# Idle identity products on TensorE in the planned waits at the start of an attention-and-two-layers kernel

## The chip, the cores and the metric

The kernel runs on one core of a Trainium2 chip. The metric is the device time of one execution in microseconds (us). Three runs of the kernel before took 609.23, 608.94 and 610.55 us, a median of 609.23. One further execution was recorded by the hardware profiler; it took 610.69 us, of which 608.5 lie between its first and its last instruction (the span). All rows below come from that one.

Names of engines: PE is TensorE (PEld its weight loads), DVE is VectorE, ACT is ScalarE, POOL is GpSimd, SP is SyncE, which here only issues DMAs.

## The reference

Attention over 2 batches of 8 heads, 768 positions of 64 numbers each: every query sees the keys nearer than 16 positions and, beside them, 24 summaries of blocks of 32 (the maximum of the keys, the mean of the values). Its output, 1536 rows of 512, goes through two dense layers of 2048 hidden units, one after the other.

```python
k_sum = k.reshape(B, H, nb, block, D).max(axis=3)
v_sum = v.reshape(B, H, nb, block, D).mean(axis=3)
scores_l = scale * np.matmul(q, k.transpose(0, 1, 3, 2))      # kept where |i - j| < 16
scores_s = scale * np.einsum('bhsd,bhnd->bhsn', q, k_sum) + np.log(block)
a = softmax(concatenate([scores_l, scores_s]))                 # in short
out = np.matmul(a, np.concatenate([v, v_sum], axis=2))
...
h = x @ w_in;  g = h * np.clip(h + 3.0, 0.0, 6.0) / 6.0;  x = g @ w_out
h = x @ w_in2; g = h * np.cos(h);                         x = g @ w_out2
```

## The kernel before

Two heads make a pair; attention works on a third of the positions (256) of one pair or, later, of two pairs at a time. One such unit is: a load of q (`z`), 16 or 32 small score products (line 538, tile `s`), mask and exponent on VectorE and ScalarE (lines 551 and 559, tile `e`), a normalising product (line 579), four transposes (line 589, tile `t`) and 16 or 32 products with v (line 600, tile `o`), whose result is split into a high and a low part, `xh` and `xl`. Before a pair's first unit its k and v are loaded, block maxima of k are taken, and block means of v are summed on PE (lines 492 and 500, tiles `h` and `y`) and copied into the tile `vw` (line 418 and 416). A float32 product is two records on PE in the trace.

The dense layers take 512 tokens by four groups of hidden units; each product with a weight is three passes (lines 702 to 704 for the first product, line 778 for the second). The weights are loaded raw, split into high and low parts on ScalarE, VectorE and GpSimd (lines 653, 657, 662, then 418 and 423, tiles `cf` and `w`), and the first of this work stands between the attention units.

Every piece of work is an operation with a priority and a cost per engine (`Plan.op`). `Plan.order` (line 252) plays the schedule through by these costs and fixes on which engine and at which planned time each operation starts; `Plan.run` (line 350) then writes the instructions in that order. On the chip each engine works through its own list in order and waits on semaphores, whatever the planned times were. In the planner's clock a product takes double its cost before 5 us (`T["cold"]`). Nine products of zeros (line 429, `warm=9`) stand ahead of everything on PE.

`Plan.run` can put idle products into the planned waits of PE: where the next operation of PE is planned to start later than the last one ends, it calls `self.idle()` (line 447), a product of the 128x128 identity with its own first 64 columns into a bank of `acc` that nothing reads before it is first used. It does so for waits that begin before `T["busy"]`, and no more once that bank is in use. `busy` is 0 before the change, so none is written.

Of the kernel before, what the change touches and what calls it, by code (L numbers as in the profile page):

```python
# [62 lines left out]
def consts():  # L63
# [13 lines left out]
T = dict(  # L77
    A0=5.118, AS=1.568, mask=-8.22, kp=-14.19, qp=-15.92, lk=-15.36, lq=-11.42, lv=-4.09, vs=37.77, vss=27.87,
    vsp=-18.03, wl=-15.78, wc=-15.19, g0=20.42, gi=5.51, pp=17.22, fill=-28.29, DVE=1.348, POOL=0.572, cold=5, d0=0.9,
    warm=9, tail=1, lagq=3, nraw=3, ncf=2, n=5, w2=2, n2=3, g2=3, nz=2, nr=1, busy=0, slack=0.2, vpe=-45.26,  # L80
    avg=-8.5,
)

# [38 lines left out]
class Plan:  # L122
# [227 lines left out]
    def run(self):  # L350
        self.refine()
        left, last, spare = self.first, T["cold"], True
        for o in self.order():
            if o.eng == "PE":
                if spare and last < T["busy"]:
                    for _ in range(int((o.start - last - T["slack"]) / (0.11 if last > T["cold"] else 0.22))):
                        self.idle()
                last = o.start + o.took
                spare = spare and not any(x.cls is self.spare and x.slot == 1 for x in o.uses)
            o.fn(o.eng)  # L360
            if o.seq < self.first:
                left -= 1
                if not left:
                    self.turn()
# [494 lines left out]
```

## Time and profile before

| | |
|---|---|
| median of three runs | 609.23 us (608.94 to 610.55) |
| profiled execution | 610.69 us |
| its span | 608.5 us |
| PE busy | 587.0 us, 96% of the span |
| VectorE, GpSimd, ScalarE busy | 386.0, 348.7, 268.1 us |
| mean granted clock of PE | 0.987 |

The granted clock is the share of 2.4 GHz that PE was given; 0.50 is its lower level, 1.2 GHz. A row of a timeline gives the start from the span's beginning, the length, engine, line, operation, what is written from what, and in brackets how long the engine was idle before it and what ended that. The records of products overlap: the distance between two starts is what one costs in a row of them.

### The profile page before, as it was taken

What the parts mean: (1) busy time and instruction counts of PE and PEld (TensorE: products, weight loads), DVE (VectorE), ACT (ScalarE), POOL (GpSimd) and SP (SyncE); (2) the same over time, 40 slices, a digit from 0 to 9 for tenths busy, and PEclk for the clock granted to TensorE, in tenths of its full rate; (3) what the DMA queues carried; (4) which work ended last, traced back from release to release, by engine and by line L of the source; (5) the groups of instructions that cost most, each with busy time, mean ns of one, the idle gap of its engine ahead of it and who ended that gap; (6) DMA issues with size and microseconds to landing.
All of it is one profiled execution on the core that took longest, in us unless ns stands there. A gap on an engine that the chain in (4) does not pass through costs nothing.

```text
span 608.5 us, 9274 instructions
## 1 busy us (share of the span) xinstructions
PE 587.0 (96%) x3482; PEld 486.0 (80%) x3482; DVE 386.0 (63%) x713; ACT 268.1 (44%) x567; POOL 348.7 (57%) x365
## 2 busy tenths in 40 slices
PE   4789899999999999999999999999999999999997
PEld 3569778788888888888888888888888888888885
DVE  4589964563952258523983689856994797575462
ACT  2878786543421114201440546654662363343240
POOL 1668864475843437623688498656763577443350
PEclk9879999999999999999999999999999999999999
DMA  9979930032410004300430013302330020000112
GB/s 245 295 226 273 256 124 18 2 139 70 138 70 0 1 22 152 103 1 0 152 125 1 1 69 105 103 1 70 104 103 2 0 104 0 1 1 1 69 53 87
DMA packets 28157, 50.05 MB, mean 82 GB/s; under 512 B 14288, under 2 KB 17744, under 8 KB 28112
## 3 DMA queue, kind: packets, MB, share of 16 engines
q1 hardware_dynamic: 27968, 49.40, 25.9%
q8 instruction: 27, 0.44, 0.3%
q14 instruction: 18, 0.15, 0.1%
q10 hardware_dynamic: 144, 0.07, 0.1%
HBM read 46.31 MB, written 3.15 MB: 81 GB/s over the span
## 4 chain that ended last, share of the span: by engine, by line
PE 88%; DMA 3%; POOL 3%; DVE 2%; ACT 2%; issue 1%; SPq 1%; DVEq 0%; ACTq 0%
PE acc L778 24%; PE s L778 18%; PE h L702 8%; PE h L703 8%; PE h L704 8%; PE t L703 3%; PE o L703 3%; PE o L704 3%; PE t L704 3%; PE o L702 3%; PE t L702 3%; DMA vw<-in_v_dram 2%; PE o L600 1%; PE s L538 1%; PE t L589 1%; ACT e L559 1%
## 5 line engine op out<-in xcount | busy, mean ns | idle before, releaser
L418 POOL TENSOR_SCALAR g<-r 128x512 fp32r<-128x512 f32 (+1 forms) x81 | 61.8, 764 | 127.4 <-DVE r L738 35.3
L423 POOL TENSOR_TENSOR g<-r,g 128x512 fp32r<-128x512 f32 (+1 forms) x83 | 111.8, 1347 | 8.6 <-ACT g L416 3.1
L734 ACT ACTIVATE n<-h,bias 128x512 f32<-128x512 f32 (+1 forms) x60 | 39.4, 656 | 138.7 <-PE h L704 138.6
L778 PE MATMUL acc<-g,w 128*128 128x512 f32 (+1 forms) x432 | 96.1, 370 | 0.6 <-POOL g L423 0.6
L702 PE MATMUL h<-xh,w 128*128 128x512 f32 (+1 forms) x240 | 92.3, 384 | 2.0 <-ACT xh L416 2.0
L703 PE MATMUL h<-xl,w 128*128 128x512 f32 (+1 forms) x240 | 90.9, 379 | 0.1
L704 PE MATMUL h<-xh,w 128*128 128x512 f32 (+1 forms) x240 | 90.6, 377 | 0.0
L778 PEld LDWEIGHTS acc<-g,w 128*128 128x128 f32 x432 | 75.1, 188 | 14.2 <-POOL g L423 0.8
L738 DVE SCALAR_TENSOR_TENSOR r<-n,h 128x512 f32<-128x512 f32 (+1 forms) x60 | 38.7, 645 | 50.9 <-POOL n L746 26.2
L423 POOL TENSOR_TENSOR w<-cf,w 128x512 fp32r<-128x512 f32 x46 | 67.3, 1466 | 3.6 <-ACT w L416 1.6
L778 PE MATMUL s<-w,g 128*128 128x512 f32 x288 | 69.2, 389 | 0.0
L778 PE MATMUL acc<-w,g 128*128 128x512 f32 x288 | 69.2, 389 | 0.0
L778 PEld LDWEIGHTS s<-w,g 128*128 128x128 f32 x288 | 54.1, 188 | 11.2
L778 PEld LDWEIGHTS acc<-w,g 128*128 128x128 f32 x288 | 54.1, 188 | 11.2
L653 ACT ACTIVATE cu<-raw 128x512 f32<-128x512 f32 x64 | 42.8, 672 | 39.9 <-DVE cf L662 27.2
L662 DVE SCALAR_TENSOR_TENSOR cf<-cu,cf 128x512 uint32<-128x512 uint32 x64 | 59.4, 943 | 1.1 <-ACT cu L653 0.5
L702 PEld LDWEIGHTS h<-xh,w 128*128 128x128 f32 x240 | 45.6, 190 | 11.0 <-ACT xh L416 2.2
L418 POOL TENSOR_SCALAR w<-cf 128x512 fp32r<-128x512 f32 x44 | 33.9, 774 | 34.2 <-DVE cf L662 24.8
L657 DVE TENSOR_SCALAR cf<-raw 128x512 uint32<-128x512 uint32 x64 | 45.0, 716 | 12.4 <-POOL w L423 9.1
L703 PEld LDWEIGHTS h<-xl,w 128*128 128x128 f32 x240 | 45.7, 190 | 8.6 <-DVE xl L423 0.7
L704 PEld LDWEIGHTS h<-xh,w 128*128 128x128 f32 x240 | 45.7, 190 | 8.1
L746 POOL TENSOR_SCALAR n<-n 128x512 f32<-128x512 f32 x36 | 26.3, 730 | 38.7 <-ACT n L734 38.6
(91 smaller groups left out, 1011.5 us busy)
## 6 DMA issues: line engine op xcount, KB each, us to landing
raw<-in_w_in_dram SPq DMA_DIRECT2D x32, 512.0 KB, 4.3
raw<-in_w_out_dram SPq DMA_DIRECT2D x32, 512.0 KB, 3.5
kw<-in_k_dram SPq DMA_DIRECT2D x8, 576.0 KB, 6.1
vw<-in_v_dram SPq DMA_DIRECT2D x8, 576.0 KB, 8.4
z<-in_q_dram SPq DMA_DIRECT2D x11, 256.0 KB, 5.8
out_dram<-part SPq DMA_DIRECT2D x8, 256.0 KB, 2.0
out_dram<-kw SPq DMA_DIRECT2D x3, 256.0 KB, 2.0
z<-in_q_dram SPq DMA_DIRECT2D x2, 128.0 KB, 5.5
```

Source lines behind the costliest of these rows:

```text
L418: eng[e].tensor_scalar(out=out, in0=in_, scalar1=scale, scalar2=0.0, op0=ALU.mult, op1=ALU.add)
L423: eng[e].tensor_tensor(out=out, in0=in0, in1=in1.bitcast(F32), op=ALU.subtract)
L653: lambda e, raw=raw, u=u: nc.scalar.activation(out=u.t, in_=raw.t.bitcast(F32)[:, :, 1], func=ACTF.Prelu, scale=2.0 ** -112, alpha=2.0 ** 32),
L657: lambda e, raw=raw, f=f: eng[e].tensor_scalar(out=f.t.bitcast(U32), in0=raw.t[:, :, 0], scalar1=2.0 ** -29, scalar2=7.0, op0=ALU.mult, op ...
L662: lambda e, u=u, f=f: nc.vector.scalar_tensor_tensor(out=f.t.bitcast(U32), in0=u.t.bitcast(U32), scalar=3, in1=f.t.bitcast(U32), op0=ALU.l ...
L702: nc.tensor.matmul(out=o, lhsT=wh, rhs=hi, start=(kk == 0), stop=False)
L703: nc.tensor.matmul(out=o, lhsT=wh, rhs=lo, start=False, stop=False)
L704: nc.tensor.matmul(out=o, lhsT=wl, rhs=hi, start=False, stop=(kk == KT - 1))
L734: op({"ACT": t(fixed, 0.43)}, lambda e: nc.scalar.activation(out=out(), in_=in_(), func=func, **kw), pr, r=rd, w=wr, take=take)
L738: op({"DVE": t(0.09, 0.56)}, lambda e: nc.vector.scalar_tensor_tensor(out=out(), in0=a(), scalar=s, in1=b(), op0=o0, op1=o1), pr, r=rd, w= ...
L746: op({"POOL": t(0.16, 0.47), "DVE": t(0.07, 0.265)}, lambda e: eng[e].tensor_scalar(out=n(), in0=n(), scalar1=1.0, scalar2=-MAGIC, op0=ALU ...
L778: nc.tensor.matmul(out=o, lhsT=l, rhs=r, start=(c == 0 and z == 0), stop=(c == GS - 1 and z == 2))
```

## The change

Two numbers. `busy` becomes 40, so idle products are written into the waits that begin before 40 us of the planned clock, and their number in each wait is worked out with a length of 0.26 us (0.46 in the first wait) in place of 0.11 (0.22).

```diff
-    warm=9, tail=1, lagq=3, nraw=3, ncf=2, n=5, w2=2, n2=3, g2=3, nz=2, nr=1, busy=0, slack=0.2, vpe=-45.26,
+    warm=9, tail=1, lagq=3, nraw=3, ncf=2, n=5, w2=2, n2=3, g2=3, nz=2, nr=1, busy=40, slack=0.2, vpe=-45.26,
...
                 if spare and last < T["busy"]:
-                    for _ in range(int((o.start - last - T["slack"]) / (0.11 if last > T["cold"] else 0.22))):
+                    for _ in range(int((o.start - last - T["slack"]) / (0.26 if last > T["cold"] else 0.46))):
                         self.idle()
```

In the program this makes 42 idle products, in eight places on PE: 8 before the first score, 15 before the first transposes, 3 before the third score, 6 before the first v sums, 5 before the first products with v, 1 before the score behind the second v sums, 1 and 3 around the products with v after it. The lists of the other engines and of the DMA queue are in the same order as before.

On PE, between the first score (`s` from k and q) and the transposes of its exponents (`t` from `e`), a piece of the difference:

```order
 L538 MATMUL s_130<-kw_92,z_84 64x120
 L538 MATMUL s_131<-kw_92,z_84 64x120
+L447 MATMUL acc_125<-ident 128x64 x15
 L589 MATMUL t_128<-ident,e_98 120x128 x4
 L538 MATMUL s_130<-kw_93,z_85 64x120
```

Fifteen products now stand where PE had nothing between the last score product and the first transpose; each transpose comes behind them on PE.

On PE, at the third piece of the dense layer's work (`h` from `xh`, `xl` and the weights `w`), with the products with v (`o`) and four transposes between:

```order
 L703 MATMUL h_127<-xl_72,w_112 128x256
 L704 MATMUL h_127<-xh_69,w_112 128x256
+L447 MATMUL acc_125<-ident 128x64
 L600 MATMUL o_129<-pt_102,vw_88 64x64 x8
 L600 MATMUL o_129<-pt_103,vw_89 64x64 x8
 L589 MATMUL t_128<-ident,e_99 120x128 x4
+L447 MATMUL acc_125<-ident 128x64 x3
 L702 MATMUL h_126<-xh_69,w_111 128x256
 L703 MATMUL h_126<-xl_72,w_111 128x256
```

One idle product now stands ahead of the products with v, and three between the transposes and the next product with `xh`.

## Rows read from the trace of the kernel before

**Rows 1.** The page, part 1: busy time, share of the span, instructions.

```profile
PE 587.0 (96%) x3482; PEld 486.0 (80%) x3482; DVE 386.0 (63%) x713; ACT 268.1 (44%) x567; POOL 348.7 (57%) x365
```

**Rows 2.** Stretches: busy time per engine (instructions), granted clock, DMA share, GB/s.

```profile
0.00:19.80 19.80, 11.33 (x126) 9.43 (x130) 8.98 (x48) 6.68 (x27) 3.75 (x14) 1.00 1.02 251
19.80:26.60 6.80, 3.92 (x74) 2.53 (x66) 3.50 (x18) 6.45 (x20) 5.65 (x7) 1.00 1.04 285
26.60:33.50 6.90, 5.90 (x72) 4.49 (x73) 3.98 (x12) 4.61 (x17) 3.45 (x6) 0.51 0.99 332
33.50:40.30 6.80, 4.66 (x79) 3.51 (x79) 6.65 (x10) 4.69 (x9) 5.37 (x5) 1.00 0.51 159
40.30:47.10 6.80, 6.55 (x69) 5.73 (x71) 5.25 (x27) 5.85 (x21) 4.88 (x7) 0.50 0.78 241
47.10:80.00 32.90, 30.53 (x483) 27.04 (x479) 29.82 (x104) 27.96 (x97) 28.19 (x36) 1.00 0.94 269
80.00:608.50 528.50, 524.10 (x2594) 433.27 (x2594) 327.81 (x498) 211.89 (x382) 297.38 (x295) 1.00 0.16 55
```

The engines in these rows are PE, PEld, DVE, ACT and POOL, in this order.

**Rows 3.** Timeline of PE, 1 to 51 us.

```profile
1.06 4.21 PE L429 MATMUL h<-n 128*128 128x128 f32 x18 [1.06 <-DVE n L427]
8.34 1.08 PE L538 MATMUL s<-kw,z 64*64 64x120 f32 x16 [3.07 <-DMA z<-in_q_dram]
12.91 1.08 PE L589 MATMUL t<-ident,e 128*120 128x128 f32 x4 [3.50 <-issue]
...
20.20 0.65 PE L589 MATMUL t<-ident,e 128*120 128x128 f32 x4
...
22.24 1.05 PE L538 MATMUL s<-kw,z 64*64 64x120 f32 x32
25.04 0.69 PE L600 MATMUL o<-pt,vw 120*64 120x64 f32 x16 [1.74 <-POOL vw L418]
...
27.08 1.51 PE L492 MATMUL h<-vw,avg 96*32 96x128 f32 x24 [0.78 <-DMA vw<-in_v_dram]
29.11 1.51 PE L492 MATMUL h<-vw,avg 96*32 96x128 f32 x24 [0.52 <-DMA vw<-in_v_dram]
...
40.40 0.58 PE L702 MATMUL h<-xh,w 128*128 128x256 f32 x1 [1.99 <-ACT xh L416]
...
43.99 1.88 PE L538 MATMUL s<-kw,z 64*64 64x120 f32 x32
...
50.01 0.63 PE L589 MATMUL t<-ident,e 128*120 128x128 f32 x4
```

**Rows 4.** The chain of waits in order of time: start, us, what.

```profile
16.97 12.10 DMA vw<-in_v_dram
29.07 0.04 issue
29.11 1.51 PE h L492 x24
...
42.99 0.21 PE h L703
...
47.97 0.12 PE h L704
```

**Rows 5.** Timeline of VectorE, its two waits for PE.

```profile
31.72 0.42 DVE L420 CAST xh<-o 128x256 fp32r<-128x256 f32 x1 [0.81 <-PE o L600]
...
45.92 0.28 DVE L551 CUSTOM_DVE_ANT_0 e<-s,mask 128x120 f32<-128x120 f32 x1 [1.32 <-PE s L538]
```

**Rows 6.** Timeline of ScalarE, its wait for PE.

```profile
47.58 0.60 ACT L416 ACTIVATE xh<-o 128x512 fp32r<-128x512 f32 x1 [1.35 <-PE o L600]
```

**Rows 7.** Timeline of GpSimd, 44 to 49 us.

```profile
44.59 0.20 POOL L571 TENSOR_SCALAR sm<-sm 128x4 f32<-128x4 f32 x1
...
47.50 1.15 POOL L579 TENSOR_TENSOR e<-e,sm 128x480 f32<-128x480 f32 x1
```

**Rows 8.** The page, part 5: PE's weight loads of line 702.

```profile
L702 PEld LDWEIGHTS h<-xh,w 128*128 128x128 f32 x240 | 45.6, 190 | 11.0 <-ACT xh L416 2.2
```

## The prediction

> **What bounds the kernel now.** I read the page's engine lines first [rows 1]. TensorE (PE) is busy 96% of the span, and nothing else is near that. Then I split the span where the granted clock changes and where PE's waits end [rows 2]: from 80.0 us to the end PE is busy 524.10 of 528.50 us at the full clock. Whatever makes PE enter that long stretch earlier or later moves the end by as much, and the change only touches what lies before 40 us of the planner's clock.
>
> In the first 47 us I went through PE's timeline, row by row with the waits [rows 3]. Two things limit PE there. One is data: it waits 3.07 us for q, 3.50 before the first transposes, 1.74 for the filled v, 0.78 and 0.52 for two v loads and 1.99 for xh. The other is its clock. The granted clock reads 0.50 from 26.6 to 33.5 and again from 40.3 to 47.1 [rows 2], the lower level, 1.2 GHz. Before its first fall the column reads 1.00, but the durations contradict it: four transposes take 1.08 us at 12.91 and 0.65 at 20.20, and 16 score products take 1.08 at 8.34 where 32 take 1.05 at 22.24 [rows 3]. So PE starts at 1.2 GHz too, and reaches 2.4 at about 20 us. Both falls come after PE had waited: the first behind the 1.74 and just before the end of the 0.78, the second at the end of the 1.99 [rows 3].
>
> **The price of an idle product.** Nothing in the trace is a 128x128 by 128x64 product. The nearest row is the warm-up: 18 records (two to a product) of 128 columns in 4.21 us [rows 3], 0.468 us a product at the low level, half of it, 0.234, at the high one. With half the columns it costs between half of that and all of it. A load of 128 columns of weights takes 190 ns whatever follows [rows 8], near the 234 ns of a record, and the idle product loads the same 128 columns; so I take the upper ends, 0.468 and 0.234. (The code itself counts with 0.46 and 0.26.)
>
> **Part by part.** The added products are 8, 15, 3, 6, 5, 1, 1 and 3, 42 in all; every other instruction stands on its engine where it stood, and no DMA moves.
>
> *The 8 before the first score.* Warm-ups end at 1.06 + 4.21 = 5.27, q lets the score start at 8.34. At the low level 8 x 0.468 = 3.74, to 9.01: the score 0.67 late. If the clock rises half way, 4 x 0.468 + 4 x 0.234 = 2.81, to 8.08, in time. What waits for that score (VectorE, then ScalarE, then SyncE's next load of q) shifts with it.
>
> *The 15 before the first transposes.* The wait is 3.50. At the high level 15 x 0.234 = 3.51 just fills it; at the low one 15 x 0.468 = 7.02, and the transposes start at 5.27 + 3.74 + 1.07 + 7.02 = 17.1 instead of 12.91, 4.2 late. This is the one place where the change can do harm.
>
> *The 3, the 6 and the 5.* They stand between the second score and the first o products, 14 x 0.234 = 3.3 us, 6.6 at the low level. What they stand ahead of ends, as the next paragraph shows, in a wait for data. Between those first o products and the last of the v sums PE waits 0.78 + 0.52, and ahead of them 1.74 [rows 3]: 3.0 us of slack against 3.3, so nothing at the high level; at the low one they add to the third rival.
>
> *Why an early clock brings nothing by itself.* The DMA engines' share is 1.02, 1.04 and 0.99 in the three stretches up to 33.5 [rows 2]. In the chain of waits a v load issued at 16.97 is in flight for 12.10 us, and the v sums on PE start at 29.11, 0.04 after it lands [rows 4]. All that PE gains before 29 ends in that wait. So I put the early part at 0, from both sides: nothing gained, and a loss only if the delay is longer than the slack there (the rival below).
>
> *The first low stretch, 26.6 to 33.5.* If PE were at 2.4 GHz there, the v sums (1.51 from 29.11) would end 0.75 earlier and the o products behind them more; VectorE waited 0.81 for that o [rows 5], so 0.8 is all that can be got. But the order puts no idle product between the transposes behind the first o products and the v sums, nor between the two v loads: the plan has those waits too short, and 0.78 and 0.52 stay open, or grow. I take 0, with 0.8 as the bound.
>
> *The second low stretch, 40.3 to 47.1.* Three idle products go into the 1.99 us wait just before it: 0.7 us of work, 1.4 at most, in a wait that ends with ScalarE's xh: free. If they keep the clock up, PE does 40.4 to 47.5 faster: 9 products of 256 columns at 0.12 each instead of 0.21 [rows 4] (0.8), four transposes 0.65 instead of 1.08 (0.4), the score 1.05 instead of 1.88 (0.8): 2.0 by the end of the score. Two thirds can be used. VectorE waits 1.32 for that score [rows 5], ScalarE 1.35 for the o products behind it [rows 6]; GpSimd runs from 44.59 without a wait, and its product that ends at 48.65 feeds the transposes at 50.01 [rows 7, 3]. All three caps say 1.3. From there to 80 us the four engines are busy 85 to 93% [rows 2], PE most, so 1.3 is passed on. Bounds: 0 if the clock falls anyway, 1.3.
>
> *The two single products* (one before the score behind the second v sums, one before the o products that follow) cost 0.23 each, 0.5 in all. They fall between 33 and 38, where VectorE is busy 6.65 of 6.80 us [rows 2] and everything waits for it. Nothing, with 0.5 as the bound.
>
> **The sum.** 0 - 0 - 1.3, against the profiled execution's 610.69 (span 608.5 and 2.2 around it), is 609.4. The median of the three runs is 609.23, 1.46 below the profiled one, and the runs fall into 608.94, 609.23 and 610.55: the distance between them is about what the second low stretch is worth. If the median run had that stretch, it goes to 607.9; if it hadn't, it stays near 609.2. I take 608.8.
>
> A page says the same of the clock: the Trainium skill, "TensorE: Matmul & The Clock Gate", in Part 1, states that the moment at which the clock rises varies from run to run of the same kernel, since it isn't tied to the kernel's start. The three times are compatible with that, no row here shows the clock of more than one run. By that rule the gain of 1.3 is a gain in some runs alone, and half of it, some 608.6, would be the median's.
>
> **The rivals.**
> 1. *The clock does as before.* The idle products stream few columns for their time, the clock still falls at 27 and 40, and they only fill waits. For it: they fill 0.7 of 1.99. Then 609.2.
> 2. *The clock stays up throughout.* For it: with the five products 1.2 of the 1.74 wait is filled. Against: the unfilled waits for v. 0.8 + 1.3 = 2.1 off: 607.1 from the median, 608.6 from the profiled run.
> 3. *Slower: the idle products run at 1.2 GHz and hold up the first transposes.* The 15 decide. If the clock isn't up when they start, the transposes come 4.2 late, and ScalarE, busy 6.45 of 6.80 us behind them [rows 2], passes that on: the o products go from 25.04 to 29.2, the v sums start at 30.5 rather than 27.08, and end at 30.5 + 2 x 0.75 = 32.0 with the clock up by then or 30.5 + 2 x 1.51 = 33.5 without, where they ended at 30.62: 1.4 to 2.9 late. VectorE already waits for them, so the end moves too: 609.23 + 1.4 to 2.9 is 610.6 to 612.1, 611.4 in the middle. For it: even the warm-up, 4.21 us of dense work, didn't raise the clock for the score at 8.34, and an idle product is less dense than that. Against: now it would be at work without a break from 1.06 on, and all three rises in the trace (about 20, 33.5 and 47.1) came while PE was at unbroken work.
>
> **Chances.** Forecast (second low stretch gone, the first not) 0.42; rival 1 0.22; rival 2 0.13; rival 3 0.23. A measurement of this kernel can't tell less than about 0.3%, 1.83 us. Faster than 607.4 needs rival 2 from the median (0.08) or the forecast with a spare 0.5 (0.04): 0.12. Slower than 611.06 is the upper half of rival 3 (0.13) and a little for what I don't see (0.03): 0.16. The rest, 0.72, is no change. The range 607.2 to 611.5 leaves out the upper quarter of rival 3 and the best of rival 2; the forecast's own is 607.9 to 609.4.
>
> **What would show it.** Right: transposes before 13.2 us with idle products of about 0.23 to 0.26 ahead of them; the v sums still starting near 29.1; a granted clock of 1.00 through 40 to 47; VectorE's 1.32 and ScalarE's 1.35 waits gone; PE's long stretch from 80 unchanged in length. Wrong: idle products of 0.46 ahead of the transposes, which then start at 17; a v load that lands earlier than 29.07, since then the early clock would pay after all; or a clock that falls at 40 in spite of the three products.

## The result: 0.75% slower, and the profile after

The changed kernel takes 613.98 us (612.93 to 615.01, 4 runs) where the kernel before, beside it, takes 609.09: a ratio of 1.0075, with a 95% interval of 1.0051 to 1.0099. A second measurement, the last of the experiments, gave 1.0024 (0.9997 to 1.0051), so the size of the loss is less sure than this first one makes it look. Ratios and intervals here and below go over all the fast runs and can differ from the quotient of the two medians; one execution of the kernel before, 843.52 us in the last batch, is slow and left out. The forecast was no change at 608.8, with a range of 607.2 to 611.5. The third rival came in, and cost more than it was given. The profiled execution took 613.61 us, 2.92 more than the one of before; that one, 610.69, is slower than each of the four runs of the kernel before, so the medians lie further apart (4.89) than the two profiles.

The page's first part says that PE has more instructions, and no other engine has:

```profile
PE 599.0 (98%) x3566; PEld 498.2 (81%) x3566; DVE 386.8 (63%) x713; ACT 268.3 (44%) x567; POOL 349.5 (57%) x365
```

Against [rows 1] that is 84 records more, the 42 products, and 12.0 us more of PE's time; the span grew by 3.0. The stretches show where those 3.0 lie. I cut again where the granted clock changes; the columns are those of [rows 2].

```profile
4.90:8.35 3.45, 2.08 (x22) 1.97 (x25) 1.97 (x5) 0.00 (x0) 0.80 (x4) 1.00 1.18 290
8.35:28.80 20.45, 20.45 (x178) 17.28 (x182) 7.57 (x44) 8.53 (x37) 5.14 (x10) 0.50 0.96 249
28.80:45.90 17.10, 13.92 (x230) 11.40 (x223) 16.22 (x47) 14.26 (x36) 13.91 (x13) 1.00 0.69 226
45.90:49.30 3.40, 3.40 (x45) 2.87 (x45) 2.59 (x13) 3.40 (x17) 1.76 (x3) 0.50 0.87 237
...
83.00:611.50 528.50, 524.10 (x2594) 433.29 (x2594) 327.52 (x498) 212.01 (x382) 297.76 (x295) 1.00 0.17 56
```

From 83.0 us to the end PE does the same 2594 instructions in the same 528.50 us as from 80.0 in [rows 2]. All of the loss is made before. And there the second row is the finding: for 20.45 us PE was busy without a single gap, and the granted clock stood at 0.50, the lower level, all through. PE's timeline tells what it was busy with:

```profile
1.06 4.10 PE L429 MATMUL h<-n 128*128 128x128 f32 x18 [1.06 <-DVE n L427]
5.00 1.90 PE L447 MATMUL acc<-ident 128*128 128x64 f32 x16
8.27 1.06 PE L538 MATMUL s<-kw,z 64*64 64x120 f32 x16 [1.37 <-DMA z<-in_q_dram]
9.26 6.66 PE L447 MATMUL acc<-ident 128*128 128x64 f32 x30
15.71 1.06 PE L589 MATMUL t<-ident,e 128*120 128x128 f32 x4
16.70 1.08 PE L538 MATMUL s<-kw,z 64*64 64x120 f32 x16
17.71 1.54 PE L447 MATMUL acc<-ident 128*128 128x64 f32 x6
19.18 1.88 PE L538 MATMUL s<-kw,z 64*64 64x120 f32 x32
20.99 2.82 PE L447 MATMUL acc<-ident 128*128 128x64 f32 x12
23.74 2.79 PE L492 MATMUL h<-vw,avg 96*32 96x128 f32 x48
...
29.61 1.33 PE L447 MATMUL acc<-ident 128*128 128x64 f32 x10
30.88 0.69 PE L600 MATMUL o<-pt,vw 120*64 120x64 f32 x16
31.49 0.65 PE L589 MATMUL t<-ident,e 128*120 128x128 f32 x4
32.07 1.52 PE L492 MATMUL h<-vw,avg 96*32 96x128 f32 x48
```

An idle product costs 1.90 / 8 = 0.238 us at the high level and 6.66 / 15 = 0.44 at the low one. The clock was up at the end of the warm-up (1.00 from 4.90), so the first group took 1.90 and left 1.37 open. At 8.35, behind that wait, it fell, and the 15 ran at 0.44: the transposes start at 15.71, 2.8 later than in [rows 3]. What the next two groups stand in shows in two more rows of the kernel before:

```profile
15.85 2.03 PE L538 MATMUL s<-kw,z 64*64 64x120 f32 x32 [0.85 <-issue]
17.81 2.46 PE L492 MATMUL h<-vw,avg 96*32 96x128 f32 x48
```

The 3 (1.54 us) fill a wait of 0.85, about half their length, and the 6 stand in no wait at all: the v sums start at 23.74, 5.9 late (17.81 before), the first products with v at 30.88, 5.8 late. Only there something is given back, because the two v loads have landed and the clock is up: the second v sums end at 32.07 + 1.52 = 33.59 instead of 30.62, 3.0 late. That is as much as the span lost.

### The profile page after: what moved, and what is told of

The parts are those of the page before. It is cut to its first block, busy times and chain, and to the rows that moved or that the text cites. A ratio compares the mean times of both kernels' runs of the same rounds, so it can differ in the third digit from the quotient of the medians.

```text
span 611.5 us, 9442 instructions
## 1 busy us (share of the span) xinstructions
PE 599.0 (98%) x3566; PEld 498.2 (81%) x3566; DVE 386.8 (63%) x713; ACT 268.3 (44%) x567; POOL 349.5 (57%) x365
## 4 chain that ended last, share of the span: by engine, by line
PE 89%; POOL 3%; DVE 3%; ACT 2%; issue 1%; DMA 1%; SPq 0%; DVEq 0%; ACTq 0%; POOLq 0%
PE acc L778 24%; PE s L778 18%; PE h L702 8%; PE h L703 8%; PE h L704 8%; PE o L704 3%; PE t L704 3%; PE o L702 3%; PE t L702 3%; PE o L703 3%; PE t L703 3%; PE acc L447 2%; PE s L538 1%; PE t L589 1%; ACT e L559 1%
## 5 line engine op out<-in xcount | busy, mean ns | idle before, releaser
L418 POOL TENSOR_SCALAR w<-cf 128x512 fp32r<-128x512 f32 x44 | 33.5, 766 | 33.5 <-DVE cf L662 23.9
```

Source lines behind the costliest of these rows:

```text
L418: eng[e].tensor_scalar(out=out, in0=in_, scalar1=scale, scalar2=0.0, op0=ALU.mult, op1=ALU.add)
```

## The experiments

All edits are against the changed kernel; counts are in the order of its eight places. Some of them move the lines by one to four: the idle product is then line 448 or 451, the v sums 493 or 496, and so on. Ratios are to the kernel before, run beside each of three batches: its median was 609.66 beside the kernels with 128 columns everywhere, without the 15, with the 15 alone and counted with 0.46; 610.0 beside those with the first group wide, without the 3 and 6, with the 8 alone and the fit; 610.34 beside the two with 60 products, the 8 with 7 more and the changed kernel again. Each profile is of one execution.

**Does the width of the idle product matter?**

```diff
-    pl.idle = lambda: nc.tensor.matmul(out=c_acc.tiles[1][:, 0:SUB], lhsT=ident, rhs=ident[:, 0:SUB], start=True, stop=True)
+    pl.idle = lambda: nc.tensor.matmul(out=c_acc.tiles[1][:, 0:P], lhsT=ident, rhs=ident, start=True, stop=True)
```

> The idle products stream all 128 columns of the identity instead of 64; their number and places stay (8, 15, 3, 6, 5, 1, 1, 3). Theory A (the 64-column products are too thin to lift PE's clock, so they run at 1.2 GHz, 0.44 us each, and the 15 hold up the first transposes): the weight load sets a product's length, so it costs the same 0.44 to 0.47 low and about 0.24 high, but now the clock is up before the 15 begin; transposes at 13.3 us or earlier, 607.5 to 609.5. Rival B (the planned waits are longer than the real ones, so the idle products are too many at any clock): 612 to 614 again.

610.15 us, ratio 1.0009 (0.9992 to 1.0026): the loss is gone, the gain isn't there. PE's timeline of this run:

```profile
5.06 2.86 PE L447 MATMUL acc<-ident 128*128 128x128 f32 x16
8.25 0.64 PE L538 MATMUL s<-kw,z 64*64 64x120 f32 x16 [0.33 <-DMA z<-in_q_dram]
8.82 3.62 PE L447 MATMUL acc<-ident 128*128 128x128 f32 x30
12.64 0.62 PE L589 MATMUL t<-ident,e 128*120 128x128 f32 x4 [0.21 <-DVE e L579]
...
26.33 0.86 PE L492 MATMUL h<-vw,avg 96*32 96x128 f32 x24 [0.27 <-DMA vw<-in_v_dram]
28.87 0.86 PE L492 MATMUL h<-vw,avg 96*32 96x128 f32 x24 [1.68 <-DMA vw<-in_v_dram]
```

The same 15 products, twice as wide, take 3.62 us instead of 6.66. And with the clock up from about 7 us on the second v sums still begin at 28.87, after 1.68 us of waiting for the load: 29.11 in [rows 4]. Rival B falls. Theory A and the prediction's "an early clock brings nothing by itself" both hold in the timeline; the time of 607.5 to 609.5 that went with theory A was missed. (The profiled execution, 608.2, is the fastest of ten.)

**A run of idle products by itself.** 60 of them before the first transposes, none elsewhere, over 64 and over 128 columns; one run each, so their times say nothing but that 60 products stood in the way. In the piece of the edit shown, `self.groups` counts the places and `idle` takes the number of columns.

```diff
+                        n, c = [(0, 64), (60, 64), (0, 64), (0, 64), (0, 64), (0, 64), (0, 64), (0, 64)][self.groups]
+                        for _ in range(n):
+                            self.idle(c)
```

> 60 idle products over 64 columns in the one place before the first transposes, none elsewhere: an unbroken run of them, measured by itself. Theory A: the clock doesn't rise in it, 60 x 0.44 = 26.4 us, transposes at 36 us. Rival F (it only takes longer than with dense work): the clock rises somewhere in the run and the rest goes at 0.24, transposes at 28 or earlier.

> The same 60 over 128 columns. Theory A: the clock rises soon after their start, some 12 at 0.46 and 48 at 0.24, 17 us, transposes at 26 to 27 us. If they stay at 0.46: 27.6 us, transposes at 37, and the columns aren't what matters.

630.04 and 620.33 us. The timeline rows of the two kernels, 64 columns first:

```profile
9.50 25.86 PE L451 MATMUL acc<-ident 128*128 128x64 f32 x120
35.16 1.06 PE L593 MATMUL t<-ident,e 128*120 128x128 f32 x4
```

```profile
9.05 15.19 PE L451 MATMUL acc<-ident 128*128 128x128 f32 x120
24.07 0.60 PE L593 MATMUL t<-ident,e 128*120 128x128 f32 x4
```

60 products over 64 columns take 0.431 us each, and the transposes behind them 1.06, the price of the low level: 25.86 us of unbroken work did not raise the clock. Over 128 columns it is 0.253 in the mean and 0.60 for the transposes. There the clock rose within the run, as the stretches of that kernel show; its score had taken 0.70 us, so the clock was up just before, fell as the 60 began (0.62 is the mean of both levels) and came back:

```profile
8.50:13.00 4.50, 4.50 (x37) 4.28 (x38) 3.65 (x14) 1.62 (x8) 1.06 (x3) 0.62 1.22 298
13.00:20.00 7.00, 7.00 (x65) 7.00 (x64) 0.58 (x2) 0.00 (x0) 0.43 (x1) 1.00 0.63 153
```

This is theory A by itself, and rival F is out. At one level the product's length hardly depends on the columns (at the low one 0.431, against 0.468 for 128 columns in the warm-up [rows 3]); what the clock did differs between the two.

**Do thin products hold a clock that is up?** The first group becomes 12 of 128 columns, `(12, 128)` in the list above; the other counts and widths are the changed kernel's.

> The first group is 12 idle products over 128 columns instead of 8 over 64, enough to bring the clock up and to reach the score; all other groups stay at 64 columns. It asks whether thin products hold a clock that is up when they begin. If they hold it, the 15 take 0.24 us each, the transposes start at about 13.3 us, and the time is near that with 128 columns everywhere, 609 to 610.5. If they don't (theory A in its stronger form), the clock falls within the 15, the transposes come at 14.5 to 16, and the 3, 6 and 5 run at 0.44: 611.5 to 614.

610.2 us, ratio 1.0005 (0.9988 to 1.0021). They didn't hold it. The rows from its timeline:

```profile
8.51 0.64 PE L542 MATMUL s<-kw,z 64*64 64x120 f32 x16 [1.11 <-DMA z<-in_q_dram]
9.08 5.10 PE L451 MATMUL acc<-ident 128*128 128x64 f32 x30
13.98 1.06 PE L593 MATMUL t<-ident,e 128*120 128x128 f32 x4
...
44.88 1.05 PE L542 MATMUL s<-kw,z 64*64 64x120 f32 x32
```

The 15 begin at the high level (the score before them took 0.64) and end at the low one: 5.10 us, between 15 x 0.238 = 3.57 and 15 x 0.44 = 6.6, and the transposes take 1.06. So far as the theory said. (PE waited 1.11 us ahead of that score; whether this had a part in the fall isn't shown. In the fit below it waited 0.89, the 14 behind had 128 columns, and their transposes took 0.62.) But the time is the one that was expected if they held it, back at that of the kernel before, for transposes only 1.7 us earlier than in the profile after. The next runs show why: part of the delay is free, and the last row, the score behind 40 us, is at the high level here.

**Which group costs how much?** Four kernels: without the 15 (below); with the 15 alone, `15 if n == 15 else 0` in its place; without the 3 and the 6; and with 0.46 us a product in all places.

```diff
-                    for _ in range(int((o.start - last - T["slack"]) / (0.26 if last > T["cold"] else 0.46))):
+                    n = int((o.start - last - T["slack"]) / (0.26 if last > T["cold"] else 0.46))
+                    for _ in range(0 if n == 15 else n):
```

> The 15 idle products before the first transposes are left out, the other 27 stay. Theory A with the 15 as the main loss: transposes near 12.9 us again, the 3 and the 6 (1.5 and 2.8 us at 1.2 GHz) still delay the v sums, which have some slack: 609.5 to 611.5. Rival C (the 3, the 6 and the 5 behind it are the loss): 612.5 or more.

> Only the 15 before the first transposes are kept. Theory A: 9.4 + 15 x 0.44 = 16.0 for the transposes instead of 12.91, 3.1 late, of which the waits behind give back a part: 610.5 to 612. Rival C (the loss is spread over the later groups): 609 to 610. If all the loss is the 15: 613 or more.

> The 3 and the 6 are left out of the changed kernel, 33 products stay. The 15 alone cost 2.3 us, everything but the 15 cost 1.4. If the losses add (the 3 and the 6 stand in one line with the 15, and each of their microseconds is passed on): 611.5 to 612.5, some 2 below the changed kernel. If they are hidden behind the delay that the 15 make: 613 to 614.

> Every count is worked out with 0.46 us a product (8, 8, 2, 3, 3, 0, 0, 2). Theory A: at 0.44 us each they now fill the real waits at the low clock, so little is lost and nothing won: 609 to 610.5. Rival D (an idle product costs something beyond its own time on PE, such as slower neighbours): 611.5 or more.

| kernel | ratio (95%) | transposes | first v sums | first o | second v sums end | span |
|---|---|---|---|---|---|---|
| before | | 12.91 | 17.81 | 25.04 | 30.62 | 608.5 |
| after | 1.0075 (1.0051 to 1.0099) | 15.71 | 23.74 | 30.88 | 33.59 | 611.5 |
| without the 15 | 1.0022 (1.0007 to 1.0037) | 12.78 | 20.82 | 28.47 | 31.19 | 608.1 |
| the 15 alone | 1.0038 (1.0023 to 1.0053) | 15.95 | 20.82 | 28.04 | 32.30 | 609.1 |
| without the 3 and 6 | 1.0010 (0.9994 to 1.0026) | 15.57 | 20.45 | 27.66 | 32.38 | 609.3 |
| first group wide | 1.0005 (0.9988 to 1.0021) | 13.98 | 22.01 | 29.53 | 32.25 | 609.3 |
| counted with 0.46 | 1.0007 (0.9991 to 1.0024) | 12.86 | 19.23 | 26.24 | 29.53 | 607.9 |
| 128 columns | 1.0009 (0.9992 to 1.0026) | 12.64 | 17.35 | 24.79 | 29.73 | 606.1 |

The times are those of PE in the profiled runs; "first o" are the first products with v. Two things are to be read. First, the lateness at the first v sums adds up: 3.0 from the 15, 3.0 from the rest, 5.9 with both. Second, 2.9 us of it are free. From the first o to the end of the second v sums PE took 5.58 us before the change, since it waited for two loads and the clock was low, and 2.71 or 2.72 in the profile after, without the 15 and with the first group wide, where the loads had landed and the clock was up. So first o that are 3.4, 4.5 and 5.8 late end 0.6, 1.6 and 3.0 late. The 15 alone and the kernel without the 3 and 6 end 1.7 and 1.8 late: there PE still waits for a load or runs at the low level.

The ratios are less clear. 0.38% for the 15 alone and 0.22% for the rest make 0.60%, which the intervals can't tell from the 0.75% with both, and the second measurement of the changed kernel, 0.24%, is about that of the rest. Nor do they price the early groups alone. The score behind 40 us took 1.05, the high level, without the 15, without the 3 and 6 and with the first group wide, and there the profile after has

```profile
47.13 1.88 PE L538 MATMUL s<-kw,z 64*64 64x120 f32 x32
```

All four have the same three products over 64 columns in the last place, and a wait of 1.37 behind them. So the second low stretch comes in some executions and not in others, and the profiles of these three were spared it: their spans are 0.8 to 1.0 us better than their second v sums are late. My expectation for the kernel without the 3 and 6 (611.5 or more; 610.42 measured) reckoned with neither the free part nor this. The other three times came out within theory A's ranges (611.02 without the 15, 611.94 with the 15 alone, 609.48 counted with 0.46). Rival C falls with the 15 alone (1.0038), and D with the counts by 0.46: products that fit the waits at the low level cost nothing that can be measured.

The delay of the loads themselves is small but there. SyncE's queue in the kernel after:

```profile
17.87 0.39 SPq L450 DMA_DIRECT2D z<-in_q_dram  x1
18.30 0.49 SPq L450 DMA_DIRECT2D raw<-in_w_in_dram  x1
18.83 0.43 SPq L450 DMA_DIRECT2D raw<-in_w_out_dram  x1
19.30 0.90 SPq L450 DMA_DIRECT2D vw<-in_v_dram  x2
```

The q load waits for the second score, and the v loads stand behind it: the last of them is issued at about 19.8 rather than 16.97 [rows 4]. In the run without the 3 and 6 that is what PE then waits for:

```profile
28.86 0.86 PE L496 MATMUL h<-vw,avg 96*32 96x128 f32 x24
31.31 1.07 PE L496 MATMUL h<-vw,avg 96*32 96x128 f32 x24 [1.58 <-DMA vw<-in_v_dram]
```

**What is the second low stretch worth?** Only 8 products of 128 columns in the last place, `[(0, 64)] * 7 + [(8, 128)]`; with 7 more before the first products with v; and the best fit by the trace, 8, 14, 0, 0, 5, 0, 0, 8, all of 128 columns.

> Only 8 idle products over 128 columns, in the wait of 2 us before the product with xh at 40 us; nothing in the other places. The prediction put 1.3 us on a clock that stays at 2.4 GHz from 40 to 47. If that holds: 1.0 to 1.3 below the kernel before in the same runs. Rival E (the clock falls there only in some of the runs of the kernel before, or others set the pace behind): within 0.5 of before.

> The 8 late products over 128 columns, and 7 of them in the wait of 1.74 us before the first products with v. If the clock then also survives the waits for the v loads, the prediction's 0.8 for the first low stretch comes on top: 607.8 to 608.5. If it falls there all the same: as with the 8 alone, 0.2% below before.

> Idle products over 128 columns, in the waits that the trace has, at their length there: 8, 14, 0, 0, 5, 0, 0, 8. The clock is up from about 7 us and through 40 to 47. If the clock is worth what the prediction said for the second low stretch: 607.9 to 608.7, 1 to 1.5 below before. Rival E (the v loads and the other engines set the pace at either clock): within 0.7 of before.

609.0 us for the 8 alone, ratio 0.9979 (0.9963 to 0.9996); 608.75 with 7 more, 0.9988 (0.9973 to 1.0003); 610.05 for the fit, 1.0000 (0.9986 to 1.0014). The 8 alone beat both kernels: the one before by 0.2%, the changed one by 0.95% or 0.45%, as its first or its second ratio is taken. Their timeline and stretch:

```profile
36.98 1.95 PE L451 MATMUL acc<-ident 128*128 128x128 f32 x16
39.13 0.38 PE L706 MATMUL h<-xh,w 128*128 128x256 f32 x1 [0.20 <-ACT xh L420]
...
41.46 1.05 PE L542 MATMUL s<-kw,z 64*64 64x120 f32 x32
42.44 1.15 PE L604 MATMUL o<-pt,vw 120*64 120x64 f32 x32
```

```profile
39.00:47.10 8.10, 6.75 (x96) 5.77 (x96) 7.67 (x34) 7.93 (x30) 6.17 (x8) 1.00 0.90 272
```

They fill the wait to its last 0.20 us; the clock stays up, the score takes 1.05 instead of 1.88 [rows 3], and VectorE and ScalarE are now the busy ones. 0.21% of 610 is 1.3 us; the interval, 0.04 to 0.37%, is wide. The span of their profile, 605.9 against 608.5, is not all theirs: nothing is added ahead of 36.98, and yet the second v sums end at 28.63 + 0.86 = 29.49 rather than 30.62, with the clock up there, 1.1 us that vary from run to run. The other two got nothing more that can be told. With 7 more the score ahead of them ran at the low level in the profile (1.88), and the 7 end at 24.49 + 2.10 = 26.6, where the first o had started at 25.04; but the clock then stays up through the waits for v, and the second v sums end at 29.03 + 0.86 = 29.89, later than with the 8 alone and earlier than before. For the fit rival E came in. Why the fit, whose profile is as short (span 606.2) as that of the 8 (605.9), is no faster in the median stays open: nine of its twelve runs lie at 609.7 or above, and the profile is of one of the other three.

**The changed kernel again.**

> The changed kernel once more, for a second profile and a second ratio. If an early rise of the clock in the warm-up spared its first profile 1.9 us, a profile without that rise has the first group at 0.44 each, the score near 9 and the transposes near 16.5 to 17: 614 to 615. Ratio again 1.005 to 1.01.

613.22 us, ratio 1.0024 (0.9997 to 1.0051), below the 1.005 to 1.01 expected. Six of its ten runs lie at 613.0 to 614.2, the other four at 608.0 to 610.1. Its profile, of one of the six, is like the first: 16.34, 24.37, 31.51 and 34.23 us in the table's columns, span 612.1, the first group again at the high level (1.91 us). So the loss isn't there in every run. What spares it in four of the fourteen runs isn't shown, since none of those four was profiled; a clock that came up earlier, or the second low stretch that stayed away, would be compatible with it.

## Why the prediction was wrong, step by step

- *The price of an idle product* was right: 0.468 and 0.234 forecast, 0.43 to 0.44 and 0.238 measured, and nearly the same for 64 and 128 columns, as the choice of the upper end said. That the choice came out was in part luck: its reason set a weight load of 190 ns, a mean over the whole span and so mostly at the high level, beside the 234 ns of a record at the low one.
- *The 8 in the first wait*: right; the score started at 8.27 for 8.34. All 8 ran at the high level.
- *"Now it would be at work without a break from 1.06 on, and all three rises in the trace came while PE was at unbroken work"*: this is the step that failed. On it rested the 15 at the high level, 15 x 0.234 = 3.51 us that "just fills" the wait of 3.50, and the mere 0.23 for the third rival; measured were 6.66 us at the low level and transposes 2.8 late. There was a break, 1.37 us ahead of the score, and unbroken work is not enough with these products: in 20.45 us of work without a gap in the profile after, and in 25.86 us of nothing but them, the clock never rose, and with the first group wide a clock that was up fell among them. The row that spoke against was there and was quoted for the rival: after 4.21 us of denser warm-up the score at 8.34 was at the low level.
- *The third rival's price*: 1.4 to 2.9 us were worked out with the 15 alone, and the sentence on the 3, the 6 and the 5 said that at the low level "they add to the third rival", without adding them. They double the delay at the v sums (5.9 instead of the 3.0 with the 15 alone). The second v sums end at 33.59, against 32.0 to 33.5 worked out, so from profile to profile the rival's upper end came in (2.92). Counted from the median of before it is 4.9; 612.1 was the end of what I gave it, and the range was cut at 611.5.
- *"No DMA moves"* was true of the order only: behind the late second score the last of the two v loads was issued at about 19.8 instead of 16.97.
- *An early clock brings nothing*: right. With 128 columns the second v sums wait 1.68 us for their load, and the ratio is 1.0009.
- *The second low stretch*: 1.3 us forecast; 8 wide products there gave 0.21%, 1.3 us. But whether three thin ones hold the clock differed: it fell at 45.9 in the profile after and at about 46 in that of its repeat, and stayed up in the profiles of three other kernels with the same three.
- *The forecast, no change*, thus had the sizes about right and the condition, the clock under the 15, wrong.

The trace of the 60 products over 64 columns shows PE busy in every microsecond of 25.86 and the low level at their end. The page "TensorE: Matmul & The Clock Gate" of the Trainium skill states in Part 1 that it is sustained PE activity which releases the throttle. The run over 64 columns disagrees with the plain reading of that sentence, the one over 128 columns agrees with it; where they differ, the measurement decides.

## What to carry to other kernels

Work that is to keep a clock up must be measured for that, by itself, before its cost is counted at the high level: a busy engine in the profile isn't enough, the granted clock and the length of the first and the last of the added products are. Idle work in an in-order engine goes where the trace shows a wait, at the length of the worse clock, and not where a plan has one. Delays of several such groups add up ahead of a common slack, here 2.9 us: price them together, not one by one.

## What the runs showed of the hardware that was not expected

A float32 product of 128x128 weights with 64 columns takes nearly as long as one with 128, 0.43 to 0.44 us against 0.46 to 0.47 at the low level and 0.24 at the high one, yet in one run each 60 of the first in a row left the clock at 1.2 GHz and 60 of the second brought it to 2.4. And the clock column reads 1.00 for the whole 25.86 us of the first, because the profile holds no record of it before 41 us; the durations (1.06 us for four transposes, 0.60 to 0.65 at the high level) are what shows the level there.

```profile
20.00:28.00 8.00, 8.00 (x40) 8.00 (x39) 0.00 (x0) 0.00 (x0) 0.00 (x0) 1.00 0.00 0
```
